# Two or three shifts on GpSimd, the Gelu bias read with the activation, and a new table, in a kernel of attention and MLP

## The chip, the cores and the metric

The kernel runs on one core of a Trainium2 chip. The metric is the device time of one execution in microseconds (us), lower is better. Of the kernel before, three timed runs are at hand: 731.67, 729.99 and 730.81 us, median 730.81 us. Five engines share the core: TensorE (PE in the profile; PEld are its weight loads), VectorE (DVE), ScalarE (ACT), GpSimd (POOL) and SyncE (SP), which issues nearly all DMAs. Matmul results land in eight PSUM banks of 128 partitions by 512 f32 values.

## The reference

With x of 2048 tokens by 512, the reference adds attention and an MLP, both on the same normalized input:

```python
xn = layernorm(x)
q = (xn @ wq) as 32 heads of 16;  k = xn @ wk;  v = xn @ wv     # one key/value head for all
p = softmax(q k^T / 4) per head
A = (p v, heads side by side) @ wo
h = gelu_tanh(xn @ w1 + b1)                                      # 512 -> 1792
B = h @ w2 + b2                                                  # 1792 -> 512
out = x + A + B
```

Inputs are bf16. The softmax has 32 heads x 2048 x 2048 exponentials; they are the bulk of the work.

## The kernel before

**Tiles and units.** Scores are computed transposed, in tiles of 128 keys by 512 (query, head) columns: 2048 tiles. Three tiles make a unit; there are 683 units. The scores of a unit (line 1080, three matmuls with 32 rows each, which stand side by side in the array) go to three PSUM banks; two halves of three banks alternate, banks 6 and 7 hold the attention output pO and a work bank pM. Four heads by 16 key tiles are a group (64 tiles); after a group pO is evacuated (lines 1234 and 1201), its rows are sent through DMAs and normalized (lines 1245, 1260, 1211, 1223).

**Two ways to an exponential.** Most tiles are exponentiated on ScalarE: one instruction per unit takes the one, two or three tiles of that unit that are not marked (line 1104; each is an "exp" below). The marked tiles, "D tiles", go to VectorE: line 1135 (p1 in the code) adds a constant to the scores in PSUM and writes 16-bit integers whose bits, read as bf16, are a straight-line approximation of the exponential. Four shifted copies of it are then weighted and summed, which smooths the approximation: the shifts are by +26, +51, +77 and -26 in integer units, and each version is multiplied with its own scaled copy of V. So a D tile costs five matmuls against V (line 1148, each 32 columns wide; four such matmuls stand side by side in the array), an ordinary tile one. D tiles are gathered into batches of one to six; the letters of the string DTAB mark them, and some letters close a batch.

**The shifts.** Before, close_batch always does three steps: slot 1 = slot 0 + 26; slots 2 and 3 = slots 0 and 1 + 51; slot 0 = slot 0 - 26 in place. The middle one is one VectorE instruction over both slots (line 1188). The other two are written for GpSimd as 64-bit additions on packs of four integers, up to two tiles each (line 1155). The planner may give such an addition to VectorE instead, where GpSimd can't take it soon (line 1156). Below, these are called fallbacks.

**What sets the order.** The program lists all operations with their dependencies; a planner (schedule, in class Prog) then writes one order per engine from assumed costs, due times and tables, and each engine runs its order with semaphore waits. [...] Tables HP, YP, Q3 and QK say at which unit each piece of the projections and of the MLP is offered. The tables RH, RQ and RY say how many of such a piece's 128-row chunks are done as four matmuls of 32 rows (line 761, kind "rs") and not as four of 32 columns (line 765): an rs matmul uses the quarter of the array that a unit's three score matmuls leave free. GpSimd's additions are gated by the planner to start while VectorE reads PSUM (line 1135 and evacuations).

**The MLP.** Hidden tiles of 128 features x 512 tokens are mostly made ahead: matmuls into pM, and VectorE adds b1 on the way out (line 1314). At two places, after units 182 and 512, ScalarE loads the Gelu table, runs all Gelus of two token blocks, and loads the exp table back (lines 1336 to 1350). Nine hidden tiles of each place are made there, straight into one half of the score banks (h_late, line 747), and Gelu reads them from PSUM (line 1340). Since this skips VectorE's addition, b1 is brought in as a fifth accumulated matmul per tile:

```python
mm4(bank(bk), b1row, ident[:, ft:ft + 1].to_broadcast([P, TBW]), True, False, ...)   # h_late
```

The output tiles (out_tile, 15 of 16) accumulate the second MLP matmul, the attention projection and b2, the last as ones x b2row over 128 rows, where only row 0 of b2row is not zero; VectorE adds x (line 1392) and SyncE stores.

Of the kernel before, what the change touches and what calls it, by code (L numbers as in the profile page):

```python
# [6 lines left out]
ACT = mybir.ActivationFunctionType  # L7
# [11 lines left out]
SPL_STEPS = ((1, 0, 1, 26), (2, 0, 2, 51), (0, 0, 1, -26))  # L19
# [35 lines left out]
RH = ((0,1,0,1,0,0,1,1,1,2,1,0,0,0),(3,0,1,0,0,1,1,1,1,1,1,1,1,1),(1,0,1,1,0,0,1,0,1,2,0,1,0,0),(0,0,1,0,1,1,1,1,1,1,1,1,1,1))  # L55
RQ = ((1,1,1,1),(1,1,2,0),(0,3,0,0),(1,1,2,0))
RY = ((3,2,3,3),(6,3,3,2),(3,4,2,4),(4,1,3,5))
# [14 lines left out]
         "o": (0,), "t": (2,), "A": (0, 1), "B": (1, 2), "X": (0, 1, 2)}  # L72
CLOSE = "otABX"
DTAB = "o0t02o.2tt2o2.t.t0.00...0t0.2Aot.0t2t.o2o2..0totA.o0o02t2tt2.20.o0.ot20t000o.B0.t022ot0.o0to2.tt22o2.tt0o2.0o0o0ttot00o2o0t222t.220.t0o0o0.o0o2tt2t2t2000t2t.022o2ooo.022.tB20.20ttA.obxXxxAo0oo0B.2.tot.2o2o...t2t.to.0ooo.020..aot.to.02t0.o2A...22o20.bott..t0o20tt.2tooo0.o202t22t.2o2o.o0o222t2tt.t20222t0t.tt2o2o0t2o2o2t.20o0.to2o0t00o000o00.22o0oA.0o0tt02.0oo0.22t2o2ot2t2.2ot0t2t0t2ttt020t0o0otta.ot.o2.o..0.2o0t..t0tot2.Bo002ot20.t.0tot00o0.0oo.t2t..o222oo.02oo22t00ot.22o0to.2t020t2o00o.t022o2o0.0t00oo.o2022a2xxXX0t2t0t0o0t2t2t0oto2o2o2oot.t000o0to2t.2ot2tt0o0.oo0t00t2t2tt2o00ot2o.0o0o0t0o0.o02o022tt2.ot.b2tt0t0..ot00toB.202oot2t.0.02o2..to.0....0.o..2o2o0..tta..ooo022t0..0..."
YF = 672.43056
# [537 lines left out]
def bass_parallel_sum__grouped_kv_mqa__dense_activation_gelu__prompt_kernel(  # L613
# [941 lines left out]
```

## Time and profile before

| what | value |
|---|---|
| timed runs, median (lowest to highest) | 730.81 us (729.99 to 731.67) |
| profiled execution, its own time | 730.02 us |
| span of the profile | 728.2 us |
| granted TensorE clock, mean | 0.997 |
| first exp, last exp ends | 24.0 us, 721.4 us |
| ACT / PE / DVE / POOL busy | 712.8 / 713.9 / 691.4 / 418.2 us |

The span runs from the first to the last instruction; 1.8 us of the execution's own time lie around it. Busy time is the union of an engine's instructions, so where one instruction begins before the one ahead has ended, the overlap counts once. The mean of one instruction is its own full duration. A matmul's duration is about 0.38 us though four of them run side by side.

### The profile page before, as it was taken

The page shows a single profiled execution, that of the slowest core. Times are in us where ns is not written, and L with a number is a line of the kernel's source. Part 1 is how long each engine was busy: PE and PEld are TensorE (multiplying, and loading weights), DVE is VectorE, ACT ScalarE, POOL GpSimd, SP SyncE. Part 2 cuts the span into 40 slices and gives each one's busy share as a digit, 9 for nine tenths or more (in the row PEclk, how much of TensorE's full clock was granted, in tenths as well). Part 3 has the DMA queues.
Part 4 walks back from the last instruction along what each step waited for, and adds up shares of the span by engine and source line. Part 5 has one row for each costly group of instructions (what it writes and reads, how often), then busy time and mean ns, then how long its engine had stood idle before and what let it go on. Part 6 is the DMA issues. An engine that isn't in the chain of part 4 may idle for free.

```text
span 728.2 us, 22534 instructions
## 1 busy us (share of the span) xinstructions
PE 713.9 (98%) x9301; PEld 223.5 (31%) x9301; DVE 691.4 (95%) x1243; ACT 712.8 (98%) x757; POOL 418.2 (57%) x669
## 2 busy tenths in 40 slices
PE   7999999999999999999999999999999999999998
PEld 5333332232242323222222233222333222232332
DVE  8799999999999889999999999999999999999685
ACT  7899999999999999999999999999999999999997
POOL 8445567667665243667777754445663767755131
PEclk9999999999999999999999999999999999999999
DMA  9200101001010110110101021100101101011111
GB/s 312 72 13 18 29 9 25 17 13 29 9 40 9 28 44 18 23 34 10 30 14 32 14 48 30 28 20 9 29 7 25 27 22 25 16 40 32 26 29 39
DMA packets 36253, 23.59 MB, mean 32 GB/s; under 512 B 17768, under 2 KB 32568, under 8 KB 36152
## 3 DMA queue, kind: packets, MB, share of 16 engines
q1 hardware_dynamic: 35096, 22.12, 11.6%
q8 instruction: 74, 1.21, 0.7%
q14 instruction: 27, 0.22, 0.1%
q10 hardware_dynamic: 1056, 0.03, 0.1%
HBM read 13.28 MB, written 2.35 MB: 21 GB/s over the span
## 4 chain that ended last, share of the span: by engine, by line
ACT 55%; PE 37%; DVE 7%; DMA 1%; issue 0%; POOL 0%; SPq 0%
ACT E L1104 55%; PE pAll L1148 18%; PE pAll L1080 11%; PE pAll L765 4%; DVE Dt L1135 3%; PE pAll L747 2%; DVE Dt L1188 2%; PE pAll L741 1%; DVE stats L854 1%; DMA x_sb<-in_A_x_dram 1%; PE pAll L910 0%; PE pAll L761 0%; DVE x_sb L1314 0%; DVE qp L1280 0%; DVE Dt L1156 0%
## 5 line engine op out<-in xcount | busy, mean ns | idle before, releaser
L1104 ACT ACTIVATE E<-pAll 128x1024 bf16<-128x1024 f32 (+2 forms) x675 | 662.4, 1154 | 2.1 <-PE pAll L1080 0.6
L1155 POOL INT64_ADD Dt<-Dt x603 | 396.2, 666 | 289.9 <-DVE Dt L1135 116.2
L1135 DVE TENSOR_SCALAR Dt<-pAll 128x512 int16<-128x512 f32 (+2 forms) x570 | 394.1, 711 | 21.5 <-PE pAll L761 16.1
L1148 PE MATMUL pAll<-Dt,V 128*32 128x512 bf16 x3010 | 413.2, 383 | 0.7 <-DVE Dt L1188 0.2
L1148 PE MATMUL pAll<-E,V 128*32 128x512 bf16 x1446 | 280.1, 385 | 0.0
L1080 PE MATMUL pAll<-QT,KT 32*128 32x512 bf16 x2048 | 267.0, 384 | 5.3 <-ACT E L1104 3.6
L1188 DVE TENSOR_SCALAR Dt<-Dt 128x1024 int16<-128x1024 int16 (+4 forms) x302 | 202.4, 680 | 1.4 <-PE pAll L1148 0.7
L1080 PEld LDWEIGHTS pAll<-QT,KT 32*128 32x128 bf16 x2048 | 66.6, 90 | 273.9 <-ACT E L1104 246.7
L1148 PEld LDWEIGHTS pAll<-Dt,V 128*32 128x32 bf16 x3010 | 106.0, 94 | 114.0 <-issue 77.3
L1148 PEld LDWEIGHTS pAll<-E,V 128*32 128x32 bf16 x1446 | 65.5, 94 | 51.4 <-issue 39.7
L765 PE MATMUL pAll<-xnT,w_sb 128*32 128x512 bf16 x520 | 80.7, 383 | 0.3 <-DVE ub L1314 0.3
L1156 DVE TENSOR_SCALAR Dt<-Dt 128x1024 int16<-128x1024 int16 (+1 forms) x147 | 46.9, 341 | 0.1
L765 PE MATMUL pAll<-w_sb,x_sb 128*32 128x512 bf16 x304 | 46.5, 382 | 0.0
L765 PE MATMUL pAll<-w_sb,ub 128*32 128x512 bf16 x352 | 45.4, 382 | 0.0
L761 PE MATMUL pAll<-w_sb,ub 32*128 32x512 bf16 x96 | 36.9, 385 | 0.0
L765 PE MATMUL pAll<-wop,oTp 128*32 128x512 bf16 x192 | 34.9, 383 | 0.0
L761 PE MATMUL pAll<-w_sb,x_sb 32*128 32x512 bf16 x88 | 33.8, 384 | 0.1
L761 PE MATMUL pAll<-xnT,w_sb 32*128 32x512 bf16 x88 | 33.8, 384 | 0.1
L765 PEld LDWEIGHTS pAll<-xnT,w_sb 128*32 128x32 bf16 x520 | 20.3, 94 | 10.6 <-issue 6.8
L761 PE MATMUL pAll<-xnT,wq_sb 32*128 32x512 bf16 x60 | 23.1, 384 | 0.0
L1314 DVE TENSOR_SCALAR ub<-pAll,b1T 128x512 bf16<-128x512 f32 x28 | 20.6, 737 | 0.0
L747 PE MATMUL pAll<-xnT,w_sb 128*32 128x512 bf16 x288 | 20.3, 379 | 0.0
(135 smaller groups left out, 381.6 us busy)
## 6 DMA issues: line engine op xcount, KB each, us to landing
w_sb<-in_B_w_dram SPq DMA_DIRECT2D x2, 1792.0 KB, 13.3
OfP<-Of SPq DMA_DIRECT2D x96, 32.0 KB, 2.0
rbP<-rden_rows SPq DMA_DIRECT2D x96, 32.0 KB, 1.8
x_sb<-in_A_x_dram SPq DMA_DIRECT2D x8, 256.0 KB, 4.5
x_sb<-in_A_x_dram SPq DMA_DIRECT2D x16, 128.0 KB, 2.1
QT<-qp SPq DMA_DIRECT2D x124, 16.0 KB, 1.8
out_dram<-x_sb SPq DMA_DIRECT2D x15, 128.0 KB, 1.9
OfP<-Of SPq DMA_DIRECT2D x56, 16.0 KB, 1.8
```

The costliest lines, as they stand in the source:

```text
L741: return add("pe", lambda e: e.matmul(o, l, rh, start=start, stop=stop, **kw), r, w, occ=occ, lat=dlat[1], allow=allow, **ak)
L747: add("pe", lambda e, c=c, j=j: e.matmul(o[c, :], l[:, c], rh, start=start, stop=stop, tile_position=(0, 32 * j)), r, [(k, j) for k in w] ...
L761: add("pe", lambda e, b, c=c, j=j: e.matmul(pM, l[c, :], rh[c, :], start=False, stop=b, skip_group_check=True, tile_position=(32 * j, 0)), ...
L765: add("pe", lambda e, b, c=c, j=j: e.matmul(pM[c, :], l[:, c], rh, start=n == 0, stop=b, skip_group_check=True, tile_position=(0, 32 * j)) ...
L1080: ins = e.matmul(o, l, rh, start=True, stop=True, tile_position=(q0, 0))
L1104: o = act(lambda e: e.activation(E[:, s0:s0 + na, :], bank(b0, na).rearrange("p (a n) -> p a n", a=na), ACT.Exp, scale=LN2 / 128.0), w=[B( ...
L1135: op = dve(lambda e: e.tensor_scalar(Dt[:, s:s + n, :], bank(bk, n).rearrange("p (a n) -> p a n", a=n), float(127 * 128) + SPL_D, SPL_MIN, ...
L1148: add("pe", lambda e, a, b: e.matmul(pO[32 * j:32 * j + 32, :], V1[:, v, kt, :], rhs, start=a, stop=b, tile_position=(0, 32 * j)), r=r + [ ...
L1155: return e.int64_add(d.bitcast(dt.uint64), x.bitcast(dt.uint64), k * 0x0001000100010001 % 2 ** 64)
L1156: return e.tensor_scalar(d, x, float(k), None, ALU.add)
L1188: dve(lambda e, d=view(o, nb), q=view(i, nb), k=k: e.tensor_scalar(d, q, float(k), None, ALU.add), r=keys(i), w=keys(o), n=nb * n * TBW, m ...
L1314: dve(lambda e: e.tensor_scalar(ubs[tb % 2][:, ft, :], pM, b1T[:, ft:ft + 1], None, ALU.add), r=["b1T"], w=M4 + [ukey(tb, ft)], n=TBW + 57 ...
```

## The change

**Two or three shifts.** SPL_STEPS now has two lists of steps. The first is the old one. In the second, slots 1 and 3 are made from slot 0 by GpSimd, slot 2 from slot 0 by VectorE, and slot 0 is shifted in place by GpSimd. Five new letters in DTAB (p, u, C, D, Y) choose the second list for the batch that they close. 168 of 295 batches, with 326 tiles, now use it.

**Gelu's bias.** The nine late tiles of each place are all read one at a time, with b1 as the activation's bias; the b1 matmul in h_late is left out for them. Before, the first three were read by one instruction over three banks.

**b2.** The ones x b2row product is taken over rows 0 to 31 only, as one rs matmul in place of four 32-column ones.

**The table.** DTAB, the offer times, RH, RQ and RY come out of a new search. 621 tiles are D tiles, where 602 were; the batches are 295, where 302 were.

Line numbers from 608 to about 1320 stand one higher in the changed kernel, later ones two to four (1336 is 1338, 1340 is 1343, 1392 is 1395).

```diff
--- before.py
+++ after.py
@@ -16,7 +16,8 @@
 SPL_K = (-26, 0, 26, 51, 77)
 SPL_C = (0.39453125, 0.349609375, 0.298828125, 0.259765625, 0.2265625)
 SPL_NB = 4
-SPL_STEPS = ((1, 0, 1, 26), (2, 0, 2, 51), (0, 0, 1, -26))
+SPL_STEPS = (((1, 0, 1, 26, "p"), (2, 0, 2, 51, "d"), (0, 0, 1, -26, "p")),
+             ((1, 0, 1, 26, "p"), (2, 0, 1, 51, "d"), (3, 0, 1, 77, "p"), (0, 0, 1, -26, "p")))
 SPL_D = -107.78043958019079
 SPL_MIN = 64.0
 SWITCH = 0.1
@@ -52,9 +53,9 @@
 RS_MAX = 3.0
 RS_GAP = 0.3
 B1U = 7
...
 NE_ND_KB = (23, 19, 11, 6)
 LA = 34
 LB = 120
@@ -69,10 +70,12 @@
 LIB_OCC = 7.0
 QSP = 1
 DMASK = {".": (), "0": (0,), "2": (2,), "a": (0, 1), "b": (1, 2), "x": (0, 1, 2),
-         "o": (0,), "t": (2,), "A": (0, 1), "B": (1, 2), "X": (0, 1, 2)}
-CLOSE = "otABX"
-DTAB = "o0t02o.2tt2o2.t.t0.00...0t0.2Aot.0t2t.o2o2..0totA.o0o02t2tt2.
...
-YF = 672.43056
+         "o": (0,), "t": (2,), "A": (0, 1), "B": (1, 2), "X": (0, 1, 2),
+         "p": (0,), "u": (2,), "C": (0, 1), "D": (1, 2), "Y": (0, 1, 2)}
+CLOSE = "otABXpuCDY"
+THREE = "puCDY"
+DTAB = "o0t02o.Cp20C2o....A0p.2.p2pt2u.D.o.tu2upo0o.o..u.p2oC.0p22B.o
...
+YF = 665.95069
 Y_ALLOW = 8.0
 H_ALLOW = 5.0
 YT_ALLOW = (3,3,3,3)
@@ -84,13 +87,11 @@
 A_SEM = 0.056
 D_LAT = 0.135
 P_LAT = 0.217
-Q3 = (50.51221,7.01364,3.70429)
...
-GU = tuple((u, tbs, n, (("s", tbs[0], 0, 7), ("p", tbs[1], 5, 3), ("s", tbs[0], 7, 7), ("p", tbs[1], 8, 1), ("p", tbs[1], 9, 1),
-                         ("p", tbs[1], 10, 1), ("s", tbs[1], 0, 5), ("p", tbs[1], 11, 1), ("p", tbs[1], 12, 1), ("p", tbs[1], 13, 1)))
-           for u, tbs, n in ((182, (0, 1), 5), (512, (2, 3), 5)))
+Q3 = (13.6227,47.82283,3.39546)
...
+GU = ((182, (0, 1), 5, (('s', 0, 0, 7), ('p', 1, 5, 1), ('p', 1, 6, 1), ('p', 1, 7, 1), ('s', 0, 7, 7), ('p', 1, 8, 1), ('p', 1, 9, 1), ('p', 1, 10, 1), ('s', 1, 0, 5), ('p', 1, 11, 1), ('p', 1, 12, 1), ('p', 1, 13, 1))), (512, (2, 3), 5, (('s', 2, 0, 7), ('p', 3, 5, 1),
...
 G_LOAD = (1.588, 1.405)
 HL_ALLOW = 0.0
 UB2 = 2
@@ -1044,7 +1045,7 @@
             return gg, r // HG, r % HG
 
         is_d = [False] * NTILE
-        last_d, bsize = {}, {}
+        last_d, bsize, three = {}, {}, {}
         exps = []
 
         half = []
@@ -1174,10 +1175,10 @@
                         gg, kt, j = tile_of(t)
                         pv_mm(gg, j, v, kt, Dt[:, slot(b) + q, :].bitcast(bf), [(("D", base[b > 0] + q), b)])
 
-            for o, i, nb, k in SPL_STEPS:
+            for o, i, nb, k, eng in SPL_STEPS[three.get(batch[0][0], 0)]:
                 def keys(b):
                     return [(("D", base[b + m > 0] + q), b + m) for m in range(nb) for q in range(n)]
-                if nb == 1:
+                if eng == "p":
                     for q in range(0, n, PL_N):
                         w = min(PL_N, n - q)
                         d, x = (Dt[:, slot(b) + q:slot(b) + q + w, :].rearrange("p a n -> p (a n)") for b in (o, i))
@@ -1314,19 +1315,20 @@
             dve(lambda e: e.tensor_scalar(ubs[tb % 2][:, ft, :], pM, b1T[:, ft:ft + 1], None, ALU.add),
                 r=["b1T"], w=M4 + [ukey(tb, ft)], n=TBW + 57, allow=ev)
 
-        def h_late(tb, ft, bk):
-            mm4(bank(bk), b1row, ident[:, ft:ft + 1].to_broadcast([P, TBW]), True, False, r=["b1row", "ident"], w=[B(bk)], allow=HL_ALLOW)
+        def h_late(tb, ft, bk, one):
+            if not one:
+                mm4(bank(bk), b1row, ident[:, ft:ft + 1].to_broadcast([P, TBW]), True, False, r=["b1row", "ident"], w=[B(bk)], allow=HL_ALLOW)
             for d in range(DT):
-                mm4(bank(bk), w1_sb[:, d, ft * P:(ft + 1) * P], xnT[:, d, tb * TBW:(tb + 1) * TBW], False, d == DT - 1,
+                mm4(bank(bk), w1_sb[:, d, ft * P:(ft + 1) * P], xnT[:, d, tb * TBW:(tb + 1) * TBW], one and d == 0, d == DT - 1,
                     r=["w1"] + tr(4 * tb, 4 * tb + 4), w=[B(bk)], allow=HL_ALLOW)
 
         gelu_after = {}
 
         def gelu(parts, u):
             hold = exps[u - 3:u + 1]
-            late = [(tb, f0 + i) for kind, tb, f0, k in parts if kind == "p" for i in range(k)]
+            late = [(tb, f0 + i, k == 1) for kind, tb, f0, k in parts if kind == "p" for i in range(k)]
             for i in range(3):
-                h_late(*late[i], 3 * half[u] + i)
+                h_late(*late[i][:2], 3 * half[u] + i, late[i][2])
             m = 0
             for n, (kind, tb, f0, k) in enumerate(parts):
                 nn = k * TBW + 50 + 1200 * (G_LOAD[0] * (n == 0) + G_LOAD[1] * (n == len(parts) - 1))
@@ -1337,10 +1339,11 @@
                 else:
                     b0 = m % 3
                     assert b0 + k <= 3
-                    o = act(lambda e, uu=uu, src=bank(3 * half[u] + b0, k).rearrange("p (a n) -> p a n", a=k): e.activation(uu, src, ACT.Gelu_apprx_tanh),
-                            w=[B(3 * half[u] + b0 + i) for i in range(k)] + uk, n=nn, kind="gelu", due=0.0, after=hold)
+                    o = act(lambda e, uu=uu, src=bank(3 * half[u] + b0, k).rearrange("p (a n) -> p a n", a=k),
+                            kw=dict(bias=b1T[:, f0:f0 + 1]) if k == 1 else {}: e.activation(uu, src, ACT.Gelu_apprx_tanh, **kw),
+                            r=["b1T"], w=[B(3 * half[u] + b0 + i) for i in range(k)] + uk, n=nn, kind="gelu", due=0.0, after=hold)
                     for i in range(m + 3, min(m + 3 + k, len(late))):
-                        h_late(*late[i], 3 * half[u] + i % 3)
+                        h_late(*late[i][:2], 3 * half[u] + i % 3, late[i][2])
                     m += k
                 hold = [o]
             run = o.fn
@@ -1387,7 +1390,7 @@
         def out_tile(tb, i):
             y_mm(tb, i, Y_ALLOW, RY[tb][i])
             wo_mm(tb, i, range(NGR // 2), Y_ALLOW, RY[tb][i])
-            chunk(FT + NGR // 2, 0, ones, b2row[:], ["ones", "b2row"], Y_ALLOW)
+            chunk(1, 1, ones, b2row, ["ones", "b2row"], Y_ALLOW, (0,))
             xr, key = x_sb[:, 14 + XSL[tb, i], :], ("x", 14 + XSL[tb, i])
             dve(lambda e: e.tensor_tensor(xr, pM, xr, ALU.add), w=[key] + M4, allow=EV_ALLOW)
             store(tb, i, xr, key)
@@ -1462,6 +1465,7 @@
             if is_d[t]:
                 first, n = (t, 1) if n == 0 else (first, n + 1)
                 if n == KB or last_d[t // TPG] == t or (DTAB[t // 3] in CLOSE and not any(is_d[t + 1:t // 3 * 3 + 3])):
+                    three[first] = int(DTAB[t // 3] in THREE)
                     bsize[first], n = n, 0
 
         dlat[:] = D_LAT, P_LAT
```

How the orders differ is shown at three places. The first is ScalarE's order at the first of the two Gelu places. ub and x_sb hold the hidden tiles, pAll is PSUM. Before:

```order
L1336 ACT_TABLE_LOAD
L1336 ACTIVATE ub<-ub 128x3584
L1340 ACTIVATE x_sb<-pAll 128x1536
L1336 ACTIVATE ub<-ub 128x3584
L1340 ACTIVATE x_sb<-pAll 128x512 x3
L1336 ACTIVATE x_sb<-x_sb 128x2560
L1340 ACTIVATE x_sb<-pAll 128x512 x3
L1350 ACT_TABLE_LOAD
```

After:

```order
L1338 ACT_TABLE_LOAD
L1338 ACTIVATE ub<-ub 128x3584
L1343 ACTIVATE x_sb<-pAll,b1T 128x512 x3
L1338 ACTIVATE ub<-ub 128x3584
L1343 ACTIVATE x_sb<-pAll,b1T 128x512 x3
L1338 ACTIVATE x_sb<-x_sb 128x2560
L1343 ACTIVATE x_sb<-pAll,b1T 128x512 x3
L1353 ACT_TABLE_LOAD
```

One instruction over three banks has become three over one bank, and all nine name b1T; the other rows are the same.

The second place is VectorE's order behind the fourth evacuation of pO (the row with Of), with Dt the tiles' slots; "128x2x1024" is a shift of two slots of two tiles each, "128x1024" one slot of two tiles. Before:

```order
L1234 COPY Of<-pAll 128x512
L1135 TENSOR_SCALAR Dt<-pAll 128x512
L1188 TENSOR_SCALAR Dt<-Dt 128x2x1024 x2
L1135 TENSOR_SCALAR Dt<-pAll 128x512
L1188 TENSOR_SCALAR Dt<-Dt 128x2x512
L1314 TENSOR_SCALAR ub<-pAll,b1T 128x512
L1135 TENSOR_SCALAR Dt<-pAll 128x512 x2
L1245 RECIPROCAL den<-den 128x32
L1135 TENSOR_SCALAR Dt<-pAll 128x512
L1188 TENSOR_SCALAR Dt<-Dt 128x2x1024
```

After:

```order
L1235 COPY Of<-pAll 128x512
L1136 TENSOR_SCALAR Dt<-pAll 128x512 x2
L1315 TENSOR_SCALAR ub<-pAll,b1T 128x512
L1136 TENSOR_SCALAR Dt<-pAll 128x512
L1189 TENSOR_SCALAR Dt<-Dt 128x1536
L1136 TENSOR_SCALAR Dt<-pAll 128x512 x2
L1246 RECIPROCAL den<-den 128x32
L1136 TENSOR_SCALAR Dt<-pAll 128x512
L1189 TENSOR_SCALAR Dt<-Dt 128x3072
L1136 TENSOR_SCALAR Dt<-pAll 128x512 x2
L1157 TENSOR_SCALAR Dt<-Dt 128x1024
L1136 TENSOR_SCALAR Dt<-pAll 128x512
```

Shifts of two slots have become shifts of one slot, over batches of another size, and a fallback (line 1157) stands where none stood in this stretch.

The third place is ScalarE's order at the end of the program, the last exps before the epilogue (L1268, in the change L1269). Before:

```order
L1104 ACTIVATE E<-pAll 128x512
L1104 ACTIVATE E<-pAll 128x1536 x2
L1104 ACTIVATE E<-pAll 128x1024 x8
L1104 ACTIVATE E<-pAll 128x1536 x2
L1104 ACTIVATE E<-pAll 128x1024
L1104 ACTIVATE E<-pAll 128x1536 x2
L1104 ACTIVATE E<-pAll 128x1024
L1268 ACTIVATE Of<-Of 128x256
```

After:

```order
L1105 ACTIVATE E<-pAll 128x512
L1105 ACTIVATE E<-pAll 128x1024 x3
L1105 ACTIVATE E<-pAll 128x1536 x3
L1105 ACTIVATE E<-pAll 128x1024 x4
L1105 ACTIVATE E<-pAll 128x1536
L1105 ACTIVATE E<-pAll 128x1024
L1105 ACTIVATE E<-pAll 128x1536
L1105 ACTIVATE E<-pAll 128x1024
L1269 ACTIVATE Of<-Of 128x256
```

Six of the 17 exps shown of before take three tiles, five of the 15 shown of the change, at other places.

More of the change, by code (lines that the diff above doesn't have):

```diff
@@ L54 @@
 B1U = 7
-RH = ((0,1,0,1,0,0,1,1,1,2,1,0,0,0),(3,0,1,0,0,1,1,1,1,1,1,1,1,1),(1,0,1,1,0,0,1,0,1,2,0,1,0,0),(0,0,1,0,1,1,1,1,1,1,1,1,1,1))
-RQ = ((1,1,1,1),(1,1,2,0),(0,3,0,0),(1,1,2,0))
-RY = ((3,2,3,3),(6,3,3,2),(3,4,2,4),(4,1,3,5))
+RH = ((0,0,0,2,0,2,0,0,1,2,0,1,1,0),(3,1,0,1,0,1,1,1,1,1,1,1,1,1),(0,1,1,0,1,0,0,0,1,2,0,1,1,1),(1,1,3,0,0,1,1,1,1,1,1,1,1,1))
+RQ = ((1,1,1,1),(2,1,0,0),(0,2,0,0),(0,1,1,0))
+RY = ((3,4,2,3),(5,3,2,2),(4,7,3,3),(5,4,2,5))
 NE_ND_KB = (23, 19, 11, 6)
```

9 lines of the change are left out of this document (5 added, 4 removed).

## The prediction

> **What bounds the kernel now.** I read the busy shares and the chain of waits on the page first, then sixteen stretches of the span, then the groups by form, last the waits. Everything here is of the one profiled execution, 730.02 us; the median is 0.8 us above it.
>
> ```profile
> PE 713.9 (98%) x9301; PEld 223.5 (31%) x9301; DVE 691.4 (95%) x1243; ACT 712.8 (98%) x757; POOL 418.2 (57%) x669
> ACT 55%; PE 37%; DVE 7%; DMA 1%; issue 0%; POOL 0%; SPq 0%
> ...
> 284.02 93.29 ACT E L1104 x97
> ...
> 110.00:151.50 41.50, 41.19 (x525) 12.13 (x520) 41.50 (x74) 41.50 (x45) 28.62 (x44) 1.00 0.09 19
> 193.00:248.00 55.00, 54.19 (x789) 18.23 (x788) 51.01 (x83) 54.08 (x51) 26.72 (x42) 1.00 0.10 24
> 248.00:292.00 44.00, 43.90 (x614) 13.57 (x610) 40.13 (x74) 43.66 (x44) 16.46 (x30) 1.00 0.12 30
> 679.50:721.50 42.00, 41.91 (x602) 13.60 (x599) 30.30 (x58) 41.61 (x39) 10.61 (x18) 1.00 0.14 37
> sum 697.50, PE 691.08 PEld 210.02 DVE 669.89 ACT 693.70 POOL 399.34; mean PE 43.19 PEld 13.13 DVE 41.87 ACT 43.36 POOL 24.96
> ```
>
> In the stretches the busy times stand in the order PE, PEld, DVE, ACT, POOL. Three engines are near full at once. ScalarE is busy 693.70 of the 697.50 us between the first exp and the last, and holds 55% of the chain; one piece of it is 97 exps in 93.29 us, 0.962 us per unit, with nothing between. VectorE is idle 27.6 us, but not evenly: nothing from 110 to 151.5 us, 11.7 us in the last 42. GpSimd has room everywhere.
>
> ```profile
> PEld pAll L1080 <- ACT E L1104: 246.7, 610, 0.9
> ACT x_sb L1340 <- PE pAll L747: 1.4, 3, 0.8
> DVE Dt L1135 <- PE pAll L761: 16.1, 30, 3.7
> PEld pAll L1148 <- POOL Dt L1155: 2.5, 11, 0.3
> ```
>
> The weight loads of the scores wait 610 times for an exp to empty its banks, 246.7 us in all: TensorE fills that time with other matmuls, but its beat is given by ScalarE. So I take ScalarE as what sets the end, VectorE as its equal in places, and TensorE close behind. The matmuls wait for GpSimd 2.5 us in all.
>
> **The change part by part. ScalarE's exps.** The orders have 675 exps before and after. By tiles per exp (3, 2, 1) they are 114, 543, 18 before and 105, 542, 28 after: 19 tiles fewer.
>
> ```profile
> L1104 ACT ACTIVATE E<-pAll 128x1024 bf16<-128x1024 f32 x543 | 515.0, 1094 | 1.2 <-PE pAll L761 0.3 <-PE pAll L1080 0.2
> L1104 ACT ACTIVATE E<-pAll 128x1536 bf16<-128x1536 f32 x114 | 169.0, 1515 | 0.9 <-PE pAll L1080 0.5
> L1104 ACT ACTIVATE E<-pAll 128x512 bf16<-128x512 f32 x18 | 11.9, 661 | 0.0
> ```
>
> Busy time by count is what one adds to a line of them, 0.948, 1.482 and 0.661 us: -9 x 1.482 - 0.948 + 10 x 0.661 = **-7.7 us**. Two bounds: the mean durations differ by 0.421 and 0.433 us per tile, which gives 19 x 0.427 = -8.1 us; and if each of the ten new one-tile exps still costs a whole unit of 0.962 us, because VectorE has two tiles of that unit, it is -9 x 1.482 - 0.948 + 9.6 = -4.7 us. I take -7.7, as one-tile exps are few and stand apart.
>
> **Gelu.** Nine reads from PSUM per place, all with a bias, for six plus one over three banks.
>
> ```profile
> L1340 ACT ACTIVATE x_sb<-pAll 128x512 bf16<-128x512 f32 x12 | 6.6, 599 | 1.5 <-PE pAll L747 1.4
> L928 ACT ACTIVATE KT<-pAll,krow 128x512 bf16<-128x512 f32 x3 | 2.1, 686 | 2.0 <-PE pAll L741 2.0
> 207.67 1.45 ACT L1340 ACTIVATE x_sb<-pAll 128x1536 bf16<-128x1536 f32 x1
> 212.66 1.57 ACT L1340 ACTIVATE x_sb<-pAll 128x512 bf16<-128x512 f32 x3 [0.40 <-PE pAll L747]
> ```
>
> Three reads in a row took 1.57 us where one of three banks took 1.45, so +0.12 at each place. The one activation of this shape with a per-partition bias, on line 928, takes 0.686 us against 0.599 without: +0.087 x 18 = +1.6. Against that, banks come free one by one, and TensorE has four products per tile where it had five, so the 1.4 us that these reads wait should go. Sum **+0.4 us**; +1.8 if the wait stays, -1.2 if the bias costs nothing here.
>
> **TensorE.** In 32-column matmuls, by the orders: -72 (b1), -60 (b2), -24 (hidden), -24 (output), +16 (queries), and +76 against V, five for each of 19 tiles where there was one. That is -88. Fillers fall too, from 100 to 68, but they only stand in idle time.
>
> ```profile
> 64.14 0.21 PE pAll L1148 x4
> 63.26 0.32 PE pAll L1080 x3
> 63.59 0.00 PE pAll L761
> ```
>
> Four cost 0.21 us, so **-4.6 us**. The rs matmuls rise by 47, 15 of them for b2. In the row above one costs 0.00 behind the three scores of its unit; 375 of 379 stand right behind scores in the new order (327 of 332 before). That is their cover, and I cost them at nothing; without it each would take its own 0.38 us, 18 us in all, which the order excludes.
>
> **VectorE.** Reads of D tiles: three one-tile reads fewer, eight of two and two of three tiles more.
>
> ```profile
> L1135 DVE TENSOR_SCALAR Dt<-pAll 128x512 int16<-128x512 f32 x544 | 360.3, 681 | 19.3 <-PE pAll L761 14.0 <-PE pAll L1080 4.2
> L1135 DVE TENSOR_SCALAR Dt<-pAll 128x1024 int16<-128x1024 f32 x20 | 24.3, 1216 | 2.2 <-PE pAll L761 2.2
> L1135 DVE TENSOR_SCALAR Dt<-pAll 128x1536 int16<-128x1536 f32 x6 | 10.5, 1748 | 0.0
> 510.40 1.20 DVE Dt L1135 x2
> L1188 DVE TENSOR_SCALAR Dt<-Dt 128x2048 int16<-128x2048 int16 x128 | 86.5, 680 | 0.4
> L1188 DVE TENSOR_SCALAR Dt<-Dt 128x3072 int16<-128x3072 int16 x36 | 34.2, 950 | 0.1
> L1156 DVE TENSOR_SCALAR Dt<-Dt 128x1024 int16<-128x1024 int16 x66 | 26.4, 414 | 0.0
> L1156 DVE TENSOR_SCALAR Dt<-Dt 128x512 int16<-128x512 int16 x81 | 22.2, 281 | 0.0
> L1155 POOL INT64_ADD Dt<-Dt x603 | 396.2, 666 | 289.9 <-DVE Dt L1135 116.2 <-DVE Dt L1188 70.1 <-DVE Dt L1156 42.0
> ```
>
> Two reads of 0.681 us in a row take 1.20: in a line each instruction costs 0.08 less than its mean. The reads: -3 x 0.60 + 8 x 1.14 + 2 x 1.67 = +10.6. Line 1188 costs 0.20, 0.33, 0.60 and 0.87 for one, two, four and six tiles, and some 0.13 a tile between. The old 302 of these come to 181 us, the new 295 (142 of two slots, 153 of one) to 142: -39. But the fallbacks rise from 147 to 279: 79 more of two tiles at 0.33, 53 more of one at 0.20, +37. Of 1204 tile shifts written for GpSimd, 213 fell to VectorE before; of 1568 now, 424. So the third GpSimd shift relieves VectorE of almost nothing, and its sum is **+8.7 us**. GpSimd gets 61 additions more, +40 us at 0.66 each, which its 289.9 us of idle time takes.
>
> Does VectorE have the 8.7 us? I split both orders into sixteen parts of 43 units, the stretches above. In the seven where it is full now (from 110 to 193, from 292 to 416 and from 556 to 636 us) its work falls by 2.3 us and ScalarE's by 0.1: no gain there, and no loss. In the other nine VectorE rises by 11, 5.9 of it in the last, against 27 us of idle, and nearly all of ScalarE's gain falls there. So I cost VectorE's rise at nothing; if that cover were gone it costs the whole 8.7.
>
> **Sum**: -7.7 + 0.4 = -7.3 us; the -4.6 on TensorE and VectorE's rise lie beside it. 730.0 - 7.3 = 722.7, and 0.8 more for the median: **723.5 us**. With the bounds (-8.1 - 1.2, -4.7 + 1.8), 721.5 to 727.9.
>
> **A page that speaks against the change.**
>
> ```profile
> 310.44 0.61 POOL L1155 INT64_ADD Dt<-Dt  x1 [0.75 <-DVE Dt L1135]
> 316.94 0.97 POOL L1155 INT64_ADD Dt<-Dt  x1 [0.82 <-DVE Of L1234]
> 316.76 0.68 DVE L1188 TENSOR_SCALAR Dt<-Dt 128x2048 int16<-128x2048 int16 x1
> ```
>
> Two additions of the same size: 0.61 us beside a PSUM read, 0.97 when begun 0.18 us into a VectorE shift, so 0.36 late. VectorE's shifts and fallbacks rise from 449 to 574 while the additions rise by 61. If each of the 125 more held one addition up, GpSimd would lose 45 us, still within its idle time.
>
> The Trainium skill (SBUF — State Buffer, "Who interferes with whom") has VectorE's fast mode and GpSimd share one port pair as a lock: the later one stands still until the first is done. The trace agrees on GpSimd's side, with the 0.36 us. By the rule a shift could also wait for an addition; the 128 shifts of four tiles show a mean of 0.680 and 0.4 us of idle ahead of them all, so the planner's gating holds that off here.
>
> **The rivals.** *TensorE sets the pace* (13%). For it: 98% busy and 37% of the chain. Against it: the 610 waits for exps. Then only its -4.6 us count: 726.2 us.
>
> *The versions come late* (8%). More additions and more fallbacks put off the last matmuls of a group, and with them the evacuation. The gain is gone when each of 31 evacuations is 7.3 / 31 = 0.24 us later: 730.8 us. The 2.5 us of waits for GpSimd speak against it, its full stretches for it.
>
> *VectorE becomes the bound* (9%, the slower side). Its 27.6 us of idle time are gaps in which it waits for scores, 16.1 us behind rs matmuls alone. If such gaps stay, the 8.7 us come on top: 739.5 us. It decides from 19.0 us of idle kept in the 697.5 (669.9 + 8.7 + 19.0): from there nothing is faster. My forecast leaves it 11.6. For it: three engines full at once. Against it: the rise stands where the idle time is.
>
> The forecast holds 70%. The range goes from 720.0 us, some room below the bounds, to 728.5, which takes in the TensorE case. About 0.2% (1.5 us) is what a measurement of this kernel can tell: faster 82%, same 9%, slower 9%.
>
> **What would show it.** Right: the span near 721; exps in 105, 542 and 28 with the same durations; Gelu's PSUM reads near 0.69 us and their waits under 0.5; VectorE busy for over 97% of the time between the exps; TensorE still waiting for exps some 600 times. TensorE's case: ScalarE's idle time before exps grows by 3 us or more. Wrong: VectorE idle 19 us or more between the exps, scores waiting for VectorE well over the few waits of now, or evacuations waiting for matmuls.

## The result, and the profile after

The changed kernel took 723.29 us in the median (722.74 to 723.95), the kernel before, run beside it, 730.46 us (729.99 to 731.67). The ratio is 0.990, with a 95% interval of 0.9883 to 0.9917: 7.2 us faster. The forecast was 723.5 us. One number in the section on the change is wrong: the second list of steps serves 153 batches, not 168; their 326 tiles are right.

The profiled execution took 723.65 us, its span is 721.6 us, and the first exp starts at 24.8 us, 0.8 us later than in the one of before. In the profiles of this document (but for the two with a shaken planner) the first exp comes at 24.8 to 25.1 us where the granted clock is 0.995 and at 23.9 to 24.3 us where it is 0.997 or more, so two medians can differ by some 0.8 us without any difference between the first exp and the last. From the page of the changed kernel, the busy times and the chain by engine:

```profile
PE 708.2 (98%) x9225; PEld 221.5 (31%) x9228; DVE 699.5 (97%) x1375; ACT 706.7 (98%) x761; POOL 439.3 (61%) x730
PE 71%; ACT 21%; DVE 7%; issue 1%; DMA 0%; SPq 0%
```

The busy shares read as before, but the chain has turned over: TensorE holds 71% of it where it held 37%, ScalarE 21% where it held 55%. The experiments will show that neither share says what shortening an engine is worth.

Between the first and the last exp, busy times of the changed kernel in two of the sixteen parts and in sum (PE, PEld, DVE, ACT, POOL):

```profile
151.80:193.00 41.20, 40.54 (x499) 11.36 (x495) 41.20 (x77) 41.20 (x44) 31.49 (x45) 1.00 0.10 21
675.50:714.90 39.40, 39.40 (x558) 12.71 (x552) 35.37 (x81) 39.07 (x39) 13.98 (x25) 1.00 0.12 32
sum 690.10, PE 685.31 PEld 207.51 DVE 677.31 ACT 687.50 POOL 420.31; mean PE 42.83 PEld 12.97 DVE 42.33 ACT 42.97 POOL 26.27
```

All of the gain lies here: 697.5 us have become 690.1. VectorE's idle time fell from 27.6 to 12.8 us, and the last part, where it had 11.7, is 39.4 us long and leaves it 4.0.

The groups on which the sum rested, first ScalarE's exps of the kernel before, then those of the changed kernel, and then its waits:

```profile
L1104 ACT ACTIVATE E<-pAll 128x1024 bf16<-128x1024 f32 (+2 forms) x675 | 662.4, 1154 | 2.1 <-PE pAll L1080 0.6
L1105 ACT ACTIVATE E<-pAll 128x1024 bf16<-128x1024 f32 (+2 forms) x675 | 654.9, 1133 | 2.5 <-PE pAll L762 1.0
L1343 ACT ACTIVATE x_sb<-pAll,b1T 128x512 bf16<-128x512 f32 x18 | 11.1, 702 | 0.0
L1157 DVE TENSOR_SCALAR Dt<-Dt 128x1024 int16<-128x1024 int16 x145 | 57.9, 417 | 0.0
L1157 DVE TENSOR_SCALAR Dt<-Dt 128x512 int16<-128x512 int16 x134 | 35.2, 283 | 0.0
L1156 POOL INT64_ADD Dt<-Dt x664 | 417.1, 638 | 260.5 <-DVE Dt L1136 84.1 <-DVE Dt L1189 68.1 <-DVE Dt L1157 49.4
```

```profile
PEld pAll L1081 <- ACT E L1105: 250.8, 623, 0.8
DVE Dt L1136 <- PE pAll L762: 8.0, 15, 1.8
PEld pAll L1149 <- POOL Dt L1156: 5.1, 23, 0.2
```

The 675 exps were busy for 662.4 us in all before, now for 654.9: -7.5. That proves less than it seems: the exps fill nearly all of the loop, so their busy time falls with the loop whatever shortens it. The Gelu reads with a bias take 0.702 us and wait for nothing. VectorE's waits behind rs matmuls have halved, from 16.1 to 8.0 us. Matmuls wait for GpSimd 5.1 us, from 2.5.

By parts of 43 units, the length of each (from the first exp of a part to the first of the next) changed as the table shows, beside the change of work that I had counted from the orders for the forecast (us):

| part | ScalarE counted | VectorE counted | TensorE counted | length measured |
|---|---|---|---|---|
| 1 to 4 | -1.7, +1.3, -0.9, 0.0 | +0.9, +0.8, -1.3, -0.7 | +0.2, +0.4, -1.2, +1.8 | -1.0, +1.4, -0.9, -0.2 |
| 5 to 8 | -0.6, -1.3, +0.4, -0.4 | +1.7, -0.5, +0.3, -0.9 | -1.6, -1.4, +0.8, -0.4 | -1.3, -1.2, +0.4, -0.3 |
| 9 to 12 | +0.4, +0.4, -2.1, -0.6 | +0.4, +1.7, -0.1, +0.3 | +0.7, +1.3, -2.1, +0.3 | +0.9, +0.9, -2.0, -0.8 |
| 13 to 16 | 0.0, +0.4, -0.4, -2.6 | -0.5, +0.4, +0.1, +5.9 | -2.4, +0.4, -0.6, -2.8 | -0.3, +0.8, -1.2, -2.5 |

TensorE's column takes in the fillers, 32 fewer, and so sums to -6.6 and not to the -4.6 of the forecast. The measured column follows ScalarE's part by part, and has the sign of TensorE's in 13 of the 16. That looks like proof that ScalarE sets the time. The first experiment shows that it isn't. One thing in it is as forecast: the seven parts in which VectorE was full (3, 4, 7 to 9, 13 and 14) changed by +0.4 us together, and the other nine carry the whole gain.

### The profile page after: what moved, and what is told of

It is laid out like the page before. It is cut to its first block, busy times and chain, and to the rows that moved or that the text cites. A ratio compares the mean times of both kernels' runs of the same rounds, so it can differ in the third digit from the quotient of the medians.

```text
span 721.6 us, 22593 instructions
## 1 busy us (share of the span) xinstructions
PE 708.2 (98%) x9225; PEld 221.5 (31%) x9228; DVE 699.5 (97%) x1375; ACT 706.7 (98%) x761; POOL 439.3 (61%) x730
## 3 DMA queue, kind: packets, MB, share of 16 engines
q1 hardware_dynamic: 35096, 22.12, 11.7%
## 4 chain that ended last, share of the span: by engine, by line
PE 71%; ACT 21%; DVE 7%; issue 1%; DMA 0%; SPq 0%
PE pAll L1149 36%; PE pAll L1081 22%; ACT E L1105 20%; PE pAll L766 8%; DVE Dt L1136 3%; PE pAll L748 3%; DVE Dt L1189 1%; PE pAll L742 1%; DVE stats L855 1%; PE pAll L911 1%; DMA x_sb<-in_A_x_dram 0%; DVE ub L1315 0%; DVE Of L1235 0%; PE pAll L762 0%; PE pAll L1519 0%
## 5 line engine op out<-in xcount | busy, mean ns | idle before, releaser
L1105 ACT ACTIVATE E<-pAll 128x1024 bf16<-128x1024 f32 (+2 forms) x675 | 654.9, 1133 | 2.5 <-PE pAll L762 1.0
L1156 POOL INT64_ADD Dt<-Dt x664 | 417.1, 638 | 260.5 <-DVE Dt L1136 84.1
L1136 DVE TENSOR_SCALAR Dt<-pAll 128x512 int16<-128x512 f32 (+1 forms) x577 | 406.6, 723 | 11.5 <-PE pAll L762 8.0
L1189 DVE TENSOR_SCALAR Dt<-Dt 128x1024 int16<-128x1024 int16 (+5 forms) x295 | 162.7, 563 | 0.4
L1157 DVE TENSOR_SCALAR Dt<-Dt 128x1024 int16<-128x1024 int16 (+1 forms) x279 | 90.2, 353 | 0.0
L766 PE MATMUL pAll<-xnT,w_sb 128*32 128x512 bf16 x496 | 69.3, 383 | 0.3 <-DVE mT L1295 0.3
L766 PE MATMUL pAll<-w_sb,ub 128*32 128x512 bf16 x332 | 54.3, 382 | 0.1
L762 PE MATMUL pAll<-w_sb,ub 32*128 32x512 bf16 x116 | 44.6, 384 | 0.2
L762 PE MATMUL pAll<-xnT,w_sb 32*128 32x512 bf16 x112 | 43.0, 384 | 0.0
L766 PE MATMUL pAll<-xnT,wq_sb 128*32 128x512 bf16 x212 | 21.4, 383 | 0.0
L748 PE MATMUL pAll<-xnT,w_sb 128*32 128x512 bf16 x288 | 19.7, 380 | 0.0
```

The source lines that it names most:

```text
L748: add("pe", lambda e, c=c, j=j: e.matmul(o[c, :], l[:, c], rh, start=start, stop=stop, tile_position=(0, 32 * j)), r, [(k, j) for k in w] ...
L762: add("pe", lambda e, b, c=c, j=j: e.matmul(pM, l[c, :], rh[c, :], start=False, stop=b, skip_group_check=True, tile_position=(32 * j, 0)), ...
L766: add("pe", lambda e, b, c=c, j=j: e.matmul(pM[c, :], l[:, c], rh, start=n == 0, stop=b, skip_group_check=True, tile_position=(0, 32 * j)) ...
L1105: o = act(lambda e: e.activation(E[:, s0:s0 + na, :], bank(b0, na).rearrange("p (a n) -> p a n", a=na), ACT.Exp, scale=LN2 / 128.0), w=[B( ...
L1136: op = dve(lambda e: e.tensor_scalar(Dt[:, s:s + n, :], bank(bk, n).rearrange("p (a n) -> p a n", a=n), float(127 * 128) + SPL_D, SPL_MIN, ...
L1156: return e.int64_add(d.bitcast(dt.uint64), x.bitcast(dt.uint64), k * 0x0001000100010001 % 2 ** 64)
```

## The experiments

All of them start from the changed kernel but one. Where the text says "in its own order", the planner plans as for the changed kernel, and the edit acts only when instructions are written out, so that every engine runs the same order and nothing but the named work differs.

### One engine made shorter at a time

Theory: ScalarE's exps set the time, the other two engines lie beside. Rivals: TensorE does, VectorE does, or all three hold each other. ScalarE made shorter:

```diff
-  o = act(lambda e: e.activation(E[:, s0:s0 + na, :], bank(b0, na).rearrange("p (a n) -> p a n", a=na),
+  nc_ = TBW if u < 40 else 504
+  o = act(lambda e: e.activation(E[:, s0:s0 + na, 0:nc_], bank(b0, na).rearrange("p (a n) -> p a n", a=na)[:, :, 0:nc_],
```

> The changed kernel in its own order, with exps that from unit 40 on read and write 504 of each tile's 512 columns (the last eight columns keep values of earlier tiles, so part of the exponentials is left out). 1341 tiles are 8 columns shorter; at 0.427 us per 512 columns that takes 0.0067 us from each, 8.9 us from ScalarE. Theory ScalarE (its beat sets the time): 7 to 9 us faster than the changed kernel, about 715 us. Rival TensorE (71% of the chain of the changed kernel): at most 1 us faster. Rival lockstep (three engines equally full, none alone decides): 2 to 4 us faster.

Measured: 722.06 us, ratio to the kernel before 0.9889 (0.9874 to 0.9904). That is 1.2 us less than the changed kernel, and the intervals overlap. The theory that ScalarE's work alone sets the time fell here; so did the 2 to 4 us that I had given the lockstep. The page of this run, the busy times and the chain:

```profile
PE 707.7 (98%) x9228; PEld 222.9 (31%) x9228; DVE 698.8 (97%) x1375; ACT 703.9 (98%) x761; POOL 438.2 (61%) x730
PE 83%; DVE 9%; ACT 6%; issue 1%; DMA 1%; SPq 0%
```

8.9 us of work were taken from ScalarE and its busy time fell by 2.8. Its groups, of this run, tell why:

```profile
L1106 ACT ACTIVATE E<-pAll 128x1008 bf16<-128x1008 f32 x516 | 482.5, 1027 | 2.4 <-PE pAll L762 0.9 <-PE pAll L1081 0.8
```

An exp of two tiles lasts 1.03 us here, but the next begins before it has ended: where nothing holds them, exps of two tiles start 0.890 us apart in this run, and 0.904 us apart in the changed kernel. So a gap of 0.1 us and more between two exps is covered by the tail of the first, and the engine reads as busy through it. The same 28 exps of ScalarE's timeline, of the changed kernel and then of this run:

```profile
109.31 26.72 ACT L1105 ACTIVATE E<-pAll 128x1024 bf16<-128x1024 f32 x28
109.22 26.67 ACT L1106 ACTIVATE E<-pAll 128x1008 bf16<-128x1008 f32 x28
```

They have 0.37 us less to do (56 tiles), take 0.05 us less, and no idle time is shown. 98% busy was no measure of how full ScalarE was. The starts are a better one. Take the exps of two and three tiles, and add up how much later than at the closest spacing of its kind the next exp starts (the Gelu places aside): 7.6 us in the changed kernel, 15.1 us here. ScalarE is held up for 7.5 us more, so most of the 8.9 us has come back as waiting.

TensorE made shorter:

```diff
-  e.matmul(pO[32 * j:32 * j + 32, :], V1[:, v, kt, :], rhs, start=a, stop=b, ...)
+  cut = lambda x, a, b: x if a or b else x[:, 0:496]
+  e.matmul(cut(pO[32 * j:32 * j + 32, :], a, b), V1[:, v, kt, :], cut(rhs, a, b), start=a, stop=b, ...)
```

> The changed kernel in its own order, with the matmuls against V taken over 496 of 512 columns, but for the first and the last of each accumulation (the contribution of the last 16 columns is left out). 4276 matmuls, four side by side in 0.21 us, are 16 columns shorter: 1069 x 0.0066 = 7.0 us off TensorE. Theory ScalarE: 0 to 1.5 us faster than the changed kernel. Rival TensorE: 5 to 7 us faster, 716 to 718 us. Rival lockstep: 2 to 4 us faster.

Measured: 721.70 us, ratio 0.9882 (0.9867 to 0.9897), 1.6 us less than the changed kernel for 7.0 us of work; in the profiled executions 0.8 of it lies ahead of the first exp. From the page of this run:

```profile
PE 706.0 (98%) x9228; PEld 223.7 (31%) x9228; DVE 698.5 (97%) x1375; ACT 706.3 (98%) x761; POOL 438.0 (61%) x730
PE 51%; ACT 46%; DVE 1%; DMA 1%; issue 0%; POOL 0%; SPq 0%
```

TensorE, with 71% of the changed kernel's chain, is not the only bound either.

VectorE made shorter:

```diff
-  op = dve(lambda e: e.tensor_scalar(Dt[:, s:s + n, :], bank(bk, n)...,
+  nc_ = TBW if ds[0][0] < 120 else 496
+  op = dve(lambda e: e.tensor_scalar(Dt[:, s:s + n, 0:nc_], bank(bk, n)...[:, :, 0:nc_],
```

> The changed kernel in its own order, with the VectorE reads of D tiles from about unit 40 on over 496 of 512 columns (the last 16 columns keep earlier values). 587 tiles are 16 columns shorter; at 0.532 us per 512 columns that is 9.8 us off VectorE. Theory ScalarE: 0 to 2 us faster than the changed kernel. Rival VectorE: 7 to 9 us faster. Rival lockstep: 2 to 4 us faster.

Measured: 722.79 us, ratio 0.9901 (0.9886 to 0.9916), 0.5 us less for 9.8 us of work. From the page of this run:

```profile
PE 708.0 (98%) x9228; PEld 218.0 (30%) x9228; DVE 694.8 (96%) x1375; ACT 706.4 (98%) x761; POOL 438.2 (61%) x730
PE 67%; ACT 28%; DVE 4%; DMA 1%; issue 0%; SPq 0%
```

Three engines, each shortened by about 1% of the time, gave 1.2, 0.7 and 0.3 us of it between the first exp and the last. No single cut came near the 7 to 9, 5 to 7 and 7 to 9 us that one bound would have given.

### Two and three engines made shorter

The same edits together, in the same order.

> Both cuts at once, in the same order: exps from unit 40 on over 504 columns (-8.9 us of ScalarE) and matmuls against V over 496 (-7.0 us of TensorE). Alone they gave 1.2 and 1.6 us. Theory pair (ScalarE and TensorE hand the work of a unit to each other, so that each hides the other's gain): 5 to 8 us faster than the changed kernel, 715 to 718 us. Rival three-way lockstep (VectorE holds too): 2.5 to 4 us faster, 719 to 721 us. Rival of independent small gains: the sum of the two, 2.8 us.

Measured: 718.44 us, ratio 0.9837 (0.9822 to 0.9851): 4.9 us less than the changed kernel, where the two alone sum to 2.8. It lies between the pair and the three-way case, a little nearer to the pair's 5 us.

> All three cuts at once, in the same order: ScalarE -8.9 us, TensorE -7.0 us, VectorE -9.8 us; alone they gave 1.2, 1.6 and 0.5 us. Three-way lockstep: 6 to 9 us faster than the changed kernel, 714 to 717 us, clearly more than with two. Theory pair: the same as with ScalarE and TensorE cut, within 1 us. Rival, that fixed waits between the engines and not their work set the time: 3 us or less.

Measured: 714.83 us, ratio 0.9787 (0.9773 to 0.9802): 8.5 us less, as the three-way lockstep said, and 3.6 us under the cut of two. VectorE's cut, worth 0.5 us alone, is worth 3.6 once the other two are shorter. Between the first and the last exp, no single cut shortens any of the sixteen parts by more than 0.26 us, and all three together shorten each by 0.28 to 0.61 us. So in no part does one engine alone set the pace. The rival of fixed waits, 3 us or less, is out. The pairs of VectorE with ScalarE and of VectorE with TensorE were not run. From the page of this run:

```profile
PE 700.3 (98%) x9228; PEld 221.3 (31%) x9228; DVE 690.6 (97%) x1375; ACT 698.4 (98%) x761; POOL 437.8 (61%) x730
PE 69%; ACT 21%; DVE 9%; issue 1%; DMA 1%; POOL 0%; SPq 0%
```

The chain is nearly that of the changed kernel, though all three engines have 7 to 10 us less to do. The same from the traces, without what lies ahead of the first exp (changes against the changed kernel, us):

| work taken from | by count | change of the median | change from first exp to last | exps held up, of two and three tiles |
|---|---|---|---|---|
| none (changed kernel) | | | (690.1) | 7.6 |
| ScalarE | -8.9 | -1.2 | -1.2 | 15.1 |
| TensorE | -7.0 | -1.6 | -0.7 | 6.5 |
| VectorE | -9.8 | -0.5 | -0.3 | 7.2 |
| ScalarE and TensorE | -8.9, -7.0 | -4.9 | -4.3 | 12.3 |
| all three | -8.9, -7.0, -9.8 | -8.5 | -7.8 | 8.7 |

The last column shows the mechanism: a faster ScalarE alone is held up more, and with each further engine made faster the hold-ups go. The 7.8 us are more than the 7.0 that I had counted for TensorE; its busy time fell by 7.9.

### ScalarE made longer

```diff
-  ACT.Exp, scale=LN2 / 128.0),
+  ACT.Exp, scale=LN2 / 128.0, **(dict(bias=zcol[:, 0:1]) if u % 8 == 5 else {})),
```

> The changed kernel in its own order, with a bias column of zeros given to the exp of every eighth unit, 85 exps. By the Gelu reads, which took 0.702 us with a bias and 0.599 without, each should take 0.09 to 0.10 us longer, 7.4 to 8.7 us in all; the output is unchanged. Theory ScalarE: 6 to 9 us slower than the changed kernel, 729 to 732 us. Rival TensorE: 0 to 2 us slower. Rival lockstep: 4 to 9 us slower, as any engine that is made longer holds the others up.

Measured: 728.70 us, ratio 0.9982 (0.9972 to 0.9991), 5.4 us slower than the changed kernel. By groups of this run, exps of two tiles without and with the bias:

```profile
L1106 ACT ACTIVATE E<-pAll 128x1024 bf16<-128x1024 f32 x475 | 460.1, 1121 | 1.0 <-PE pAll L763 0.4 <-PE pAll L1082 0.2
L1106 ACT ACTIVATE E<-pAll,zcol 128x1024 bf16<-128x1024 f32 x67 | 80.0, 1194 | 0.3 <-PE pAll L1082 0.3
```

And its chain:

```profile
ACT 74%; PE 24%; DVE 1%; DMA 1%; issue 0%; SPq 0%
```

The longer ones last 0.073 us more, but a duration holds the covered gaps too. From start to start it is 0.996 us behind an exp of two tiles with the bias and 0.903 behind one without (medians), so 0.093 us each and 7.9 us for 85, as I had priced it. Between the first exp and the last, 5.9 us of the 7.9 show. That fits the lockstep's 4 to 9 us and falls just short of the 6 to 9 of ScalarE alone; by itself this run would hardly separate the two. With the cuts it does: making one engine longer costs most of what it is longer, making it shorter gives little. And the chain, which gave ScalarE 21%, now gives it 74% after a change of about 1%.

### The two small edits undone, in the same order

Gelu's bias undone, b1 added by matmuls again:

```diff
-  mm4(bank(bk), w1_sb[...], xnT[...], one and d == 0, d == DT - 1, ...)
+  mm4(bank(bk), w1_sb[...], xnT[...], False, d == DT - 1, ..., first=(b1row, ident[...]) if d == 0 else None)   # b1 product in front
-  kw=dict(bias=b1T[:, f0:f0 + 1]) if k == 1 else {}
+  kw={}
```

> The changed kernel in its own order, with Gelu's bias undone: the 18 reads from PSUM carry no bias, and b1 goes back in as a fifth product in front of each of the 18 late tiles (72 matmuls, +3.8 us of TensorE, all inside the two Gelu places). ScalarE gets 18 x 0.10 = 1.8 us back. Theory that ScalarE sets the pace inside the Gelu places: 0.5 to 1.8 us faster than the changed kernel, about 722 us, as long as the reads do not wait for TensorE. Rival TensorE paces there: the waits of these reads return (1.4 us before) and the 3.8 us show, 1 to 3 us slower.

Measured: 726.55 us, ratio 0.9948 (0.9932 to 0.9965), 3.3 us slower than the changed kernel; just past the rival's 1 to 3. ScalarE's timeline around the first Gelu place, of the changed kernel:

```profile
212.12 1.85 ACT L1343 ACTIVATE x_sb<-pAll,b1T 128x512 bf16<-128x512 f32 x3
213.83 2.37 ACT L1338 ACTIVATE x_sb<-x_sb 128x2560 bf16<-128x2560 bf16 x1
216.06 1.87 ACT L1343 ACTIVATE x_sb<-pAll,b1T 128x512 bf16<-128x512 f32 x3
```

And of this run:

```profile
212.37 1.08 ACT L1346 ACTIVATE x_sb<-pAll 128x512 bf16<-128x512 f32 x2 [0.51 <-PE pAll L750]
213.34 2.34 ACT L1341 ACTIVATE x_sb<-x_sb 128x2560 bf16<-128x2560 bf16 x1
215.61 0.60 ACT L1346 ACTIVATE x_sb<-pAll 128x512 bf16<-128x512 f32 x1
217.54 0.60 ACT L1346 ACTIVATE x_sb<-pAll 128x512 bf16<-128x512 f32 x1 [1.33 <-PE pAll L750]
218.40 0.60 ACT L1346 ACTIVATE x_sb<-pAll 128x512 bf16<-128x512 f32 x1 [0.27 <-PE pAll L750]
```

Each read is 0.1 us shorter, and the reads wait for TensorE: 0.51, 1.33 and 0.27 us here. The part with the first Gelu place is 1.95 us longer; the second place and the part behind it 1.8 us. So the bias buys TensorE's time with less of ScalarE's, at the two places where TensorE is late. In all, these reads wait 3.5 us here, against 1.4 us in the kernel before, whose order was made for five products: part of the cost may be that of an order made for four.

b2 undone, the four 32-column matmuls in place of the rs matmul:

```diff
+  if l is ones:      # behind the rs matmul of b2: write four column matmuls in its place
+      pr.ops[-1].fn = four      # ones[:, q] x b2row over 128 rows, q = 32-column pieces
```

> The changed kernel in its own order, with b2 undone: at the same 15 places four 32-column matmuls over 128 rows stand where one rs matmul over rows 0 to 31 stands. TensorE gets 15 x 0.21 = 3.2 us more, behind the scores. Theory lockstep (a longer engine holds the others up, as 85 longer exps cost 5.4 of some 8 us): 1.5 to 3.5 us slower than the changed kernel, 725 to 727 us. Rival, that the 32-row matmul was free and so is its undoing because TensorE waits for exps anyway: within 0.7 us.

Measured: 725.09 us, ratio 0.9926 (0.9912 to 0.9941), 1.8 us slower for 3.2 us more of TensorE, inside the lockstep's range (2.6 us between the first exp and the last). The column form is not free. That fits an rs form under the scores' cover, but no run left the rs matmuls out, so that it costs nothing is not shown.

### The third shift on VectorE

```diff
-  dve(lambda e, ...: e.tensor_scalar(d, q, float(k), None, ALU.add),
+  dve(lambda e, ...: (x is not None and e.tensor_scalar(x[:, 0:TBW], q2, float(k), None, ALU.add),   # one tile, spare buffer
+                      e.tensor_scalar(d, q, float(k), None, ALU.add))[1],
```

> The changed kernel in its own order, but in each of the 153 batches that give two shifts of slot 0 to GpSimd beside the in-place one, VectorE does one more shift of one tile into a spare buffer, so that it bears part of what the third shift took from it; GpSimd's work stays. 153 x 0.20 = 30.6 us more of VectorE, which has 12.9 us of idle time between the exps. Had the third shift been left to VectorE for all 326 tiles, it would be some 43 us. Theory lockstep: 18 to 30 us slower than the changed kernel, 741 to 753 us, so the table of 621 D tiles needs the third shift. Rival, the reading that the third shift relieves VectorE of almost nothing and VectorE lies beside the path: under 5 us.

Measured: 747.90 us, ratio 1.0239 (1.0222 to 1.0257), 24.6 us slower than the changed kernel for 30.6 us. From the page of this run, and then two of the waits of its exps, which wait 2.5 us in all in the changed kernel:

```profile
PE 724.7 (97%) x9225; PEld 229.9 (31%) x9228; DVE 726.0 (97%) x1528; ACT 719.6 (97%) x761; POOL 457.1 (61%) x730
DVE 49%; PE 46%; ACT 3%; issue 2%; DMA 1%; POOL 0%; SPq 0%
```

```profile
ACT E L1106 <- PE pAll L763: 4.6, 19, 0.5
ACT E L1106 <- PE pAll L1082: 4.4, 14, 0.8
```

VectorE could take 6 us of it. 621 D tiles without the third shift on GpSimd are out of reach for VectorE in this order. The run keeps the 279 fallbacks and all of GpSimd's additions; without the third shift GpSimd would have had room for some of the fallbacks. So 24.6 us is what 30.6 us more on VectorE cost, and not what the third shift is worth.

### The planner's constant shaken

Here the planner plans anew, with one latency changed by a nanosecond, in the changed kernel and in the one before:

```diff
-D_LAT = 0.135
+D_LAT = 0.136
```

> The changed kernel with one assumed latency of the planner (VectorE to its readers) 0.136 us and not 0.135. The work is the same, 621 D tiles and 675 exps of the same sizes, but the planner's orders come out another way: 164 fillers for 68, 310 fallbacks for 279. Theory of work (the sums of work set the time): within 1.5 us of the changed kernel. Rival fit (the table is fitted to one exact order, and the time hangs on the fit): 3 to 8 us slower, 726 to 731 us.

> The kernel before with the same latency of the planner 0.136 us and not 0.135. The work is the same as before; fillers rise from 100 to 424, fallbacks from 147 to 211. Theory of work: within 1.5 us of the kernel before. Rival fit: 5 to 15 us slower, 735 to 745 us; then the step from before to the change, both shaken, tells what is gained without the fit: if it is 7 us again, the work carries the gain, if it is near 0 or far off, the fit does.

Measured: 768.34 us, ratio 1.0508 (1.0487 to 1.0530), and 813.59 us, ratio 1.1146 (1.1128 to 1.1163). Nearly the same work, 45 and 83 us slower; far past what I had priced from the fillers. Both shaken, the step from before to the change is 45 us and not 7, so that comparison says nothing of what the work alone is worth. The waits of ScalarE, of the shaken changed kernel, then of the shaken kernel before:

```profile
ACT x_sb L1338 <- DVE x_sb L1315: 16.5, 1, 16.5
ACT ub L1512 <- PE pAll L748: 16.3, 1, 16.3
ACT E L1105 <- PE pAll L1081: 9.6, 10, 5.6
```

```profile
ACT E L1104 <- PE pAll L761: 42.5, 9, 20.0
ACT ub L1336 <- DVE ub L1314: 16.9, 1, 16.9
```

They are few and long: a Gelu place that waits 16.5 us for one hidden tile, the end that waits 16.3 us for the last output. I read this so, without a test of its own: the offer times are set so tightly that side work which slips a little misses its date, and then the whole program stands. Therefore the third shift, the table and the two edits can't be priced by taking one away and planning anew: such a kernel would show the lost fit.

The last run planned with 0.136 us again and searched the tables anew, in small random steps, for that constant:

```diff
-DTAB = "o0t02o.Cp20C2o....A0p.2.p2pt2u.D.o.tu2upo0o.o..
+DTAB = "o0t02o.D2u0C2o....A0p.2.putp2u.D.o.uu2uoo0oto..
...
-YP = ((185.78825,206.7778,189.89434,222.39217), ...
+YP = ((184.796, 188.19, 186.043, 212.765), ...
```

In this kernel one x tile of the first token block is loaded before an earlier output tile has used the same buffer, so that tile adds another tile's x; the work is the same.

> The changed kernel with the planner's latency at 0.136 us, as in the shaken one, and its tables searched again for that constant: small random steps in DTAB, the offer times and the rs counts, kept when the planner's own order came out shorter. 95 of 683 letters differ; the work is nearly that of the changed kernel (622 D tiles for 621, 675 exps). Theory fit: most of the 45 us that the shaken kernel lost come back, 728 to 734 us, which would put the loss down to the fit of table and order and not to the constant or the work. Rival, that the other latency itself makes poor orders: 750 us or more.

Measured: 731.10 us, ratio 1.0013 (1.0004 to 1.0023). 37 of the 45 us came back with other tables alone, so the fit between table and order was lost and mostly found again. The 8 us that are left may come from the constant or from a shorter search; no run tells.

## Why the prediction was right, and where its reasons were not

The number, its sign and most signs of being right held. VectorE's rise was put at 8.7 us and its idle time at 11.6: busy +7.4, idle 12.8. "TensorE still waiting for exps some 600 times": 623. The slower rival, with 19 us of idle kept on VectorE, did not come. Nor did the versions come late: matmuls wait for GpSimd 5.1 us where they waited 2.5. The page that spoke against the change did not weigh either: the additions that overlap a shift or fallback rose by 39, not by 125, and the mean addition fell from 0.666 to 0.638 us. So GpSimd's busy time rose by 21 us where the forecast had 40.

The sum itself is right in part by luck. "Busy time by count is what one adds to a line" was a misreading, as the covered gaps show: 0.948 and 1.482 us hold waiting, and from start to start it is 0.904 and 1.330 us. Counted by starts in the two traces, the nine exps of three tiles fewer bring -12.0 us and the one-tile exps more +6.3, so the term "-7.7" is -5.7. Two smaller things make up for it. The other exps are held up 0.9 us less, and the two Gelu places bring -0.6 where the forecast had +0.4 (from the start of the last exp ahead to the first behind; the reads take 0.702 us and their wait is gone, as said).

The step that failed is the first: "I take ScalarE as what sets the end", with "the -4.6 on TensorE and VectorE's rise lie beside it". In the changed kernel 8.9 us off ScalarE alone gave 1.2, so the other two don't lie beside it. I read the gain as one of all three: in the same table TensorE fell by its 4.6 and VectorE's rise went where it had idle time; the forecast had costed both at nothing. How much of the 7.2 us the shorter exps alone would have brought in the kernel before is not shown, as the cuts were made in the changed kernel only. The rival "TensorE sets the pace" fell by the same test, at 1.6 us for 7.0.

Also too strong was "the third GpSimd shift relieves VectorE of almost nothing". I compared VectorE's shift work before and after, -39 and +37, and overlooked that the same row carries 19 more D tiles. By the forecast's own prices, shifts and fallbacks took VectorE 219 us for 602 tiles and take 217 for 621: 0.364 us a tile, now 0.349, which is some 9 us on 621 tiles. That is an estimate; and the run with 30.6 us more on VectorE shows that it had no room for more.

The cover of the rs matmuls is borne out as far as it was tried: four column matmuls in their place cost 1.8 us. The forecast put the worth of the b2 edit only under TensorE, and so at nothing; that of the b1 edit there and in the 1.4 us of waits.

How the 7.2 us divide between the third shift, the two edits and the table stays open. 3.3 and 1.8 us are what the edits are worth in an order that was fitted with them; in an order fitted without them they may be worth less. To divide the gain, each part would need a search of its own of the same depth, and the search of the last run ended 8 us above the changed kernel.

## What to carry to other kernels

When several engines are full, a busy share and a share of the chain don't name the bound: cut each engine's work by one per cent in an unchanged order, and then all of them together; only the joint cut shows what a change of everything is worth. A change that lightens one of three balanced engines gives little by itself, here 0.3 to 1.2 us for 7 to 10, so count what it does to each. Where instructions overlap their neighbours, take their price from start to start and not from busy time. And where a search has fitted a static order to exact constants, try edits in the order as it stands: planning anew cost 45 and 83 us here, where the whole change is worth 7.

## What the runs showed that was not expected

A bias column makes an activation longer by about 0.09 us: from start to start 0.996 us against 0.903 for exps of 1024 columns, by duration 0.702 against 0.595 for the Gelu reads of 512 with the bias undone. The duration of an exp is no price: the same 542 exps of 1024 columns last 1.088 us in the changed kernel, 1.123 with TensorE shortened and 1.034 with VectorE made longer. The same order runs with the same lengths again and again: with the bias undone, thirteen of the sixteen parts kept their length within 0.01 us, and only the three at and behind the Gelu places changed. What did differ between executions lay ahead of the loop, where, among the runs in the changed kernel's own order, the first exp came up to 1.3 us earlier or later.
